# Retention in front of two feed-forward blocks: attention in native float32 by chunks of 96 tokens

## The chip, the cores and the metric

One core of a Trainium2 chip runs the whole program. The metric is the device time of one execution in microseconds (us), less is better; three runs of the kernel before have a median of 931.69 us (930.37 to 932.35).

## The reference

```python
scores = (q @ k.T) / sqrt(64)                       # 4 batches, 8 heads, 576 tokens, head size 64
gamma = 1 - 2 ** (-5 - head)
ret = scores * where(row >= col, gamma ** (row - col), 0)
x = (ret @ v)                                       # heads side by side: 2304 tokens x 512
h = max(max(x @ w1, x @ w2), x @ w3)                # 512 -> 768
x2 = h @ w_out                                      # 768 -> 512
g = x2 @ w_gate                                     # 512 -> 1536
out = (g * sigmoid(g) * (x2 @ w_val)) @ w_out2      # 1536 -> 512
```

The activations are float32 and the weights float64.

## The kernel before, in words

A product in full precision is made in one of two ways. *Native*: one matmul on float32 operands, which the profile shows as two MATMUL records (passes). *In pairs*: each operand is split into a high part that is a float32r and a float32r rest, and three matmuls (high by rest, rest by high, high by high) add up in PSUM. The feed-forward blocks work in pairs throughout.

**Conversions.** Each weight block of 128 x 512 is loaded as float64 by SP's queue (`load_w`, L86; three buffers `w64`) and turned into a float32r pair by `conv_w` (L94): two ScalarE copies (L98, L99), three VectorE steps (L100 to L102), the rounding on ScalarE (L103) and a subtraction (L104), on GpSimd for the first layer's 18 blocks and on VectorE for the others.

**Attention** works in 32 units of (batch, half of the sequence, pair of heads), halves being 256 and 320 tokens. The causal part within a half is computed over triangles of blocks (`BLK`); what the first half adds to the second goes through one 64 x 64 state per head. A unit goes through four functions:
- `a_load` (L118) loads q, k and v; from unit 12 on, q and k come in a form that VectorE can transpose.
- `a_prep` (L151) transposes q and k (TensorE L164 up to unit 11, then VectorE L168, L169), scales q by powers of the decay rate, and from unit 8 on (`NF`) splits all into float32r pairs on ScalarE, VectorE and GpSimd (L185 to L208).
- `a_score` (L211), for one head: matmuls L232, then decay and mask on VectorE (L237), then the split (L246 to L251).
- `a_value` (L254), for one head: matmuls L288, evacuation (L294 to L300, L329, L330) to the pair xh, xl, and in a first half the state (L306 to L325).

Units 0 to 7 are native. One head's matmuls use 64 of the array's 128 rows or columns; the other head's come after them.

**First layer.** `f_slice` (L357) makes a slice: 12 matmuls (L366) for one half batch, one block of 128 of h and one of the three weights, into one of three PSUM banks (`ps_mm`, L74). ScalarE copies the first of three to `hmax` (L370), VectorE takes the maximum with the other two (L372), and the result is written to DRAM (L374). There are 18 slices a half batch, 144 in all.

**Order.** The loop over the units (L405) emits preparation two units ahead, scores one ahead, values, up to three conversions for each of the first six units, and between them 4 or 5 slices a unit (`quota`, L409) from a queue that gets a half batch's 18 slices when its four units are done (L406). The last half batch's 18 slices stand behind the loop (L474 to L480), with the first conversions for the next layers. The Tile framework puts the instructions of every engine, TensorE's too, in an order by a simulated timeline, so an engine's order may leave the program's.

**Behind it**: x2 = h @ w_out by half batches, h being loaded again and split (`h_split`, L463; L498), and the second block (`gate_val` L513, `out2` L537). Both take their products from the same three `ps_mm` banks, the second block's last product from five of its own.

Of the kernel before, what the change touches and what calls it, by code (L numbers as in the profile page):

```python
# [21 lines left out]
P = 128  # L22
NP = H // 2
CH = ((0, 256), (256, 320))
C = 320
# [5 lines left out]
BLK = (((0, 128), (128, 128)), ((0, 128), (128, 128), (256, 64)))  # L31
# [3 lines left out]
O_ID, O_MK, O_SC, O_KS, O_G = 0, 128, 448, 472, 488  # L35
NCONST = O_G + NP * C


def _constants():
    """Identity, causal mask and powers of the heads' decay rates: shapes alone."""  # L40
    c = np.zeros((P, NCONST), np.float64)
    gam = 1.0 - 2.0 ** (-5.0 - np.arange(H))
    p = np.arange(P)
    m = np.arange(C)
    c[:, O_ID:O_MK] = np.eye(P)
    c[:, O_MK:O_SC] = m[None, :] >= p[:, None]
    g = np.zeros((P, NP, C))
    for pr in range(NP):
        g[:D, pr] = gam[2 * pr] ** m
        g[D:, pr] = gam[2 * pr + 1] ** m  # L50
    c[:, O_G:NCONST] = g.reshape(P, -1)
    j = 128.0 * np.arange(3)[None, :, None] + p[:, None, None]
    c[:, O_SC:O_KS] = (gam ** (-j) / np.sqrt(D)).reshape(P, -1)
    c[:, O_KS:O_G] = (gam ** (CH[0][1] - j[:, :2]) / np.sqrt(D)).reshape(P, -1)
    return c.astype(np.float32)
# [3 lines left out]
def retention_moe(ctx, tc, consts, q, k, v, w1, w2, w3, w_out, w_gate, w_val, w_out2, out):  # L59
# [14 lines left out]
    ps_mm = ctx.enter_context(tc.tile_pool(name="ps_mm", bufs=3, space=PSUM))  # L74
# [4 lines left out]
    ident = cst[:, O_ID:O_MK]  # L79
    mask = cst[:, O_MK:O_SC]  # L80
    sc_t = cst[:, O_SC:O_KS].rearrange("p (j h) -> p j h", j=3)
    ks_t = cst[:, O_KS:O_G].rearrange("p (j h) -> p j h", j=2)
    g_t = cst[:, O_G:NCONST].rearrange("p (r m) -> p r m", r=NP)

# [25 lines left out]
    NF = 8   # the first units run in native float32, the others as float32r pairs  # L110
    PT = 12  # the first units transpose on TensorE, the others on VectorE
    units = [(b, c, pr) for b in range(B) for c in range(2) for pr in range(NP)]
    NU = len(units)
    U = {}
    states = {}
    xs = {}

    def a_load(n):  # L118
        if n >= NU:
            return  # L120
        b, c, pr = units[n]
        c0, cw = CH[c]
        vn = att.tile([P, 3, 2, D], F32, name="vn", tag="vn", bufs=3)
        if n < PT:
            qk = att.tile([P, 2, 3, 2, D], F32, name="qk", tag="qk", bufs=3)
            kn = qk[:, 1, 0:2]
            nat_ld = ((qk[:, 0], q), (qk[:, 1], k), (vn, v))
        else:
            qk = att.tile([P, 2, C // 32, 32], F32, name="qk", tag="qk", bufs=3)[:, :, 0:cw // 32]
            for i, s in enumerate((k, q)):  # L130
                for e in range(2):
                    for x in range(2):
                        g = 64 * e + 32 * x
                        sp.dma_start(out=qk[g:g + 32, 1 - i],  # L134
                                     in_=s[b, 2 * pr + e, c0:c0 + cw, 32 * x:32 * x + 32].rearrange("(a p) d -> p a d", p=32))
            nat_ld = ((vn, v),)
            kn = None
            if c == 0:
                kn = att.tile([P, 2, 2, D], F32, name="kn", tag="kn", bufs=2)
                nat_ld = ((kn, k), (vn, v))  # L140
# [113 lines left out]
    def a_value(n, e):  # L254
        if n >= NU or n < 0:
            return
# [334 lines left out]
```

## Time and profile before

| | us |
|---|---|
| median of three runs | 931.69 |
| span of the profiled execution | 931.2 |
| TensorE busy (matmuls) | 898.6 |
| VectorE busy | 559.5 |
| ScalarE busy | 400.0 |
| GpSimd busy | 286.6 |

The profile gives for the profiled execution its span, from the first instruction to the last; it is the same as the runs' time within 0.5 us. Engines work beside one another, so their busy times don't add up to the span. Matmul records are pipelined and overlap: a matmul's cost is the distance from its start to the next one's start, not the length of its record. PE is TensorE's matmuls, PEld its weight loads, DVE VectorE, ACT ScalarE, POOL GpSimd, SP SyncE.

### The profile page before, as it was taken

How to read it: one execution, taken by the hardware profiler on the slowest of the kernel's cores; microseconds unless marked ns; L12 is line 12 of the kernel's file. 1: busy time of each engine (PE TensorE's matmuls, PEld its weight loads, DVE VectorE, ACT ScalarE, POOL GpSimd, SP SyncE). 2: the span in 40 equal slices, each digit the busy share in tenths (PEclk: the TensorE clock that was granted, in tenths of full speed). 3: DMA queues.
4: the chain of work that ended last, by engine and by line, in shares of the span. 5: the costliest groups of instructions: out<-in, count | busy, mean ns of one | idle time of the engine just before them, and what ended most of it. 6: DMA issues, size and time to landing. Idle time of an engine off the chain costs nothing.

```text
span 931.2 us, 14346 instructions
## 1 busy us (share of the span) xinstructions
PE 898.6 (96%) x5208; PEld 783.6 (84%) x5208; DVE 559.5 (60%) x1088; ACT 400.0 (43%) x892; POOL 286.6 (31%) x294
## 2 busy tenths in 40 slices
PE   6998988999998999999999999999999999999998
PEld 4776887989998999999988888888888888888887
DVE  3699999999999975941171154375366343333333
ACT  3666665665665755744363253143133122111111
POOL 2465435544544553144411111112111111111111
PEclk9999999999999999999999999999999999999999
DMA  7775453333232104752240021021011000000112
GB/s 174 205 209 179 86 129 67 72 70 72 62 72 61 31 25 130 236 147 83 65 130 7 1 91 45 1 91 46 1 61 53 1 1 1 1 0 1 46 68 92
DMA packets 131640, 67.79 MB, mean 73 GB/s; under 512 B 92528, under 2 KB 126960, under 8 KB 131568
## 3 DMA queue, kind: packets, MB, share of 16 engines
q1 hardware_dynamic: 131568, 66.87, 26.1%
q8 instruction: 41, 0.67, 0.3%
q14 instruction: 31, 0.25, 0.1%
HBM read 55.04 MB, written 11.80 MB: 72 GB/s over the span
## 4 chain that ended last, share of the span: by engine, by line
PE 66%; DVE 3%; DMA 2%; issue 1%; ACT 1%; SPq 0%; POOL 0%; DVEq 0%; ACTq 0%; POOLq 0%
PE ps L523 33%; PE ps L545 16%; PE ps L366 8%; PE ps L498 8%; PE o_ps L288 1%; PE s L232 1%; DMA w<-in_moe_w_val_dram 1%; DMA w<-in_moe_w_out_dram 0%; DMA qk<-in_q_dram 0%; SPq L134 0%; DVE hmax L372 0%; DVE wz L101 0%; DMA hf<-h_d 0%; DVE rq L196 0%; DVE pf L237 0%
## 5 line engine op out<-in xcount | busy, mean ns | idle before, releaser
L534 POOL TENSOR_TENSOR gl<-gf,gh 128x512 fp32r<-128x512 f32 (+1 forms) x60 | 74.7, 1245 | 385.8 <-ACT gh L533 385.8
L366 PE MATMUL ps<-xl,wh 128*128 128x256 f32 (+1 forms) x576 | 178.5, 311 | 14.7 <-DVE hmax L372 13.1
L523 PE MATMUL ps<-x2h,wrl 128*128 128x512 f32 (+1 forms) x480 | 179.1, 373 | 0.0
L523 PE MATMUL ps<-x2l,wrh 128*128 128x512 f32 (+1 forms) x480 | 179.1, 373 | 0.0
L523 PE MATMUL ps<-x2h,wrh 128*128 128x512 f32 (+1 forms) x480 | 179.1, 373 | 0.0
L366 PE MATMUL ps<-xh,wlo 128*128 128x256 f32 (+1 forms) x576 | 172.3, 299 | 0.0
L366 PE MATMUL ps<-xh,wh 128*128 128x256 f32 (+1 forms) x576 | 172.3, 299 | 0.0
L366 PEld LDWEIGHTS ps<-xl,wh 128*128 128x128 f32 x576 | 109.8, 191 | 23.2 <-DVE hmax L372 16.1
L531 DVE TENSOR_TENSOR sg<-ps,sg 128x512 f32<-128x512 f32 (+1 forms) x60 | 38.2, 637 | 125.9 <-ACT sg L530 125.7
L366 PEld LDWEIGHTS ps<-xh,wlo 128*128 128x128 f32 x576 | 110.0, 191 | 0.8 <-issue 0.8
L366 PEld LDWEIGHTS ps<-xh,wh 128*128 128x128 f32 x576 | 109.9, 191 | 0.5 <-issue 0.3
L523 PEld LDWEIGHTS ps<-x2l,wrh 128*128 128x128 f32 x480 | 90.4, 188 | 18.2
L523 PEld LDWEIGHTS ps<-x2h,wrl 128*128 128x128 f32 x480 | 90.4, 188 | 17.9
L523 PEld LDWEIGHTS ps<-x2h,wrh 128*128 128x128 f32 x480 | 90.4, 188 | 17.6
L530 ACT ACTIVATE sg<-ps 128x512 f32<-128x512 f32 (+1 forms) x60 | 33.1, 552 | 154.2 <-PE ps L523 154.1
L551 DVE TENSOR_TENSOR acc<-ps,acc 128x512 f32<-128x512 f32 x90 | 62.1, 690 | 50.7 <-PE ps L545 50.6
L247 POOL TENSOR_TENSOR pl<-pf,ph 128x384 fp32r<-128x384 f32 (+1 forms) x48 | 60.2, 1256 | 102.9 <-ACT ph L246 78.5
L533 ACT ACTIVATE gh<-gf 128x512 fp32r<-128x512 f32 (+1 forms) x60 | 35.2, 586 | 125.4 <-DVE gf L532 125.4
L545 PE MATMUL ps<-wrh,gl 128*128 128x512 f32 x216 | 85.7, 397 | 0.0
L545 PE MATMUL ps<-wrl,gh 128*128 128x512 f32 x216 | 85.5, 396 | 0.0
L545 PE MATMUL ps<-wrh,gh 128*128 128x512 f32 x216 | 85.1, 394 | 0.0
L532 DVE TENSOR_TENSOR gf<-ps,sg 128x512 f32<-128x512 f32 (+1 forms) x60 | 38.3, 638 | 65.5 <-PE ps L523 64.8
(89 smaller groups left out, 1653.7 us busy)
## 6 DMA issues: line engine op xcount, KB each, us to landing
w<-in_moe_w_dram SPq DMA_DIRECT2D x18, 512.0 KB, 4.2
w<-in_moe_w_out_dram SPq DMA_DIRECT2D x18, 512.0 KB, 4.4
w<-in_moe_w_gate_dram SPq DMA_DIRECT2D x12, 512.0 KB, 4.3
w<-in_moe_w_val_dram SPq DMA_DIRECT2D x12, 512.0 KB, 4.1
out_dram<-acc SPq DMA_DIRECT2D x18, 256.0 KB, 2.0
vn<-in_v_dram SPq DMA_DIRECT2D x64, 64.0 KB, 2.3
h_d<-hmax SPq DMA_DIRECT2D x24, 160.0 KB, 1.9
hf<-h_d SPq DMA_DIRECT2D x24, 160.0 KB, 2.5
```

Source lines behind the costliest of these rows:

```text
L232: pe.matmul(dst[i][0], lk[:, o:o + w], rq[:, o:cw], start=l == 0, stop=l == len(prods) - 1)
L247: pool.tensor_tensor(pl[:, sl], pf[:, sl], f(ph[:, sl]), ALU.subtract)
L366: pe.matmul(ps, l[:, ksl], r, start=n == 0, stop=n == 3 * KD - 1)
L498: pe.matmul(ps, l[:, es], r, start=n == 0, stop=n == 3 * F1 - 1)
L523: pe.matmul(ps[:, 0:tw], l[:, ksl], r, start=n == 0, stop=n == 3 * KD - 1)
L530: act.activation(sg[:, 0:tw], pr[0][:, 0:tw], ACTF.Sigmoid)
L531: dve.tensor_tensor(sg[:, 0:tw], pr[0][:, 0:tw], sg[:, 0:tw], ALU.mult)
L532: dve.tensor_tensor(gf[:, 0:tw], pr[1][:, 0:tw], sg[:, 0:tw], ALU.mult)
L533: act.activation(gh[:, 0:tw], gf[:, 0:tw], ACTF.Copy)
L534: pool.tensor_tensor(gl[:, 0:tw], gf[:, 0:tw], f(gh[:, 0:tw]), ALU.subtract)
L545: pe.matmul(ps, l[:, sl], r, start=n == 0, stop=n == 3 * GRP - 1)
L551: dve.tensor_tensor(a, ps, a, ALU.add)
```

## The change

- Halves are 288 and 288 tokens. Attention is native for all 32 units, now (batch, pair of heads, half), a pair's two halves one after the other. A half has three chunks of 96 tokens; scores and values are computed within a chunk, and all that came before goes through a state per chunk boundary (six states a pair, the first zero; VectorE scales the last state and adds the new product).
- Both heads' matmuls of a chunk stand one after the other in different tiles of the array: scores in the two halves of its rows, into two banks; state products and values in the two halves of its columns, into one bank. The product with the state is one matmul for both heads on a block-diagonal state.
- All transposes are on TensorE, k and q into one PSUM tile. VectorE applies decay and mask in one instruction a half and makes xl straight from PSUM.
- A pair's q, k and v (whole sequence) are loaded at once, three pairs deep. The constants come in one load.
- `ps_mm` has two banks, here and in all that follows; attention's tiles have one buffer each (six banks).
- Inside a manual schedule TensorE keeps the order in which the program emits. The slices of a batch (36, its halves alternating) join the queue when all its eight halves are done; 108 of them lie in iterations 8 to 31, the last batch's 36 behind the loop, six beside each conversion.
- `hf` has three buffers for five, `wl` two for three, `hmax` three for two, one of them held per half.

The old attention functions are left out here, as are the constants' values and comments that went.

```diff
-CH = ((0, 256), (256, 320))
-C = 320
+CK = 96
+NC = 3
+C = CK * NC
+CH = ((0, C), (C, C))
...
-O_ID, O_MK, O_SC, O_KS, O_G = 0, 128, 448, 472, 488
-NCONST = O_G + NP * C
+O_ID = 0
+O_D = O_ID + CK
+O_G = O_D + NP * 2 * CK
+O_KS = O_G + NP * CK
+O_E = O_KS + NP * 2
+NCONST = O_E + NP
...
-    ps_mm = ctx.enter_context(tc.tile_pool(name="ps_mm", bufs=3, space=PSUM))
+    ps_mm = ctx.enter_context(tc.tile_pool(name="ps_mm", bufs=2, space=PSUM))
...
-        l = stg.tile([P, 512], U32, name="wl", tag="wl")
+        l = stg.tile([P, 512], U32, name="wl", tag="wl", bufs=2)
...
+    halves = [(b, pr, h) for b in range(B) for pr in range(NP) for h in range(2)]
+    NU = len(halves)
     U = {}
     xs = {}
+    stz = [att.tile([P, 2 * NC, 2, D], F32, name=f"stz{i}", tag=f"stz{i}", bufs=1) for i in range(2)]
+    for t in stz:
+        pool.memset(t, 0.0)
+    def a_load(u):
+        if u >= B * NP:
+            return
+        b, pr = divmod(u, NP)
+        t = {}
+        for nm, s in (("k", k), ("q", q), ("v", v)):
+            t[nm] = att.tile([CK, 2 * NC, 2, D], F32, name=f"{nm}n", tag=f"{nm}n", bufs=3)
+            for e in range(2):
+                sp.dma_start(out=t[nm][:, :, e, :],
+                             in_=s[b, 2 * pr + e].rearrange("(a p) d -> p a d", p=CK))
+        U[u] = t
+    def a_prep(n):
         if n >= NU:
             return
+        b, pr, h = halves[n]
+        u = U[n // 2]
+        if h == 0:
+            ks = att.tile([CK, 2 * NC, 2, D], F32, name="ks", tag="ks")
+            sc = ks_t[:, pr].unsqueeze(1).unsqueeze(3).to_broadcast([CK, 2 * NC - 1, 2, D])
+            pool.tensor_tensor(ks[:, 0:2 * NC - 1], u["k"][:, 0:2 * NC - 1], sc, ALU.mult)
+            u["ks"] = ks
+        tp = psa.tile([P, 2, 512], F32, name="tp", tag="tp")
+        for x, nm in ((0, "k"), (1, "q")):
+            for c in range(NC):
+                pe.transpose(tp[:, x, c * CK:(c + 1) * CK],
+                             u[nm][:, h * NC + c].rearrange("p h d -> p (h d)"), ident)
+        kt = att.tile([P, C], F32, name="kt", tag="kt")
+        qg = att.tile([P, NC, CK], F32, name="qg", tag="qg", bufs=3)
+        act.activation(kt, tp[:, 0, 0:C], ACTF.Copy)
+        dve.tensor_tensor(qg, tp[:, 1, 0:C].rearrange("p (c m) -> p c m", c=NC),
+                          g_t[:, pr].unsqueeze(1).to_broadcast([P, NC, CK]), ALU.mult)
+        u[h] = {"kt": kt, "qg": qg}
+    def a_score(n):
+        if n >= NU:
+            return
+        b, pr, h = halves[n]
+        w = U[n // 2][h]
+        s = psa.tile([CK, 2, 512], F32, name="s", tag="s")
+        for c in range(NC):
+            cs = slice(c * CK, (c + 1) * CK)
             for e in range(2):
+                hd = slice(64 * e, 64 * e + 64)
+                pe.matmul(s[:, e, cs], w["kt"][hd, cs], w["qg"][hd, c], start=True, stop=True)
+        pT = att.tile([CK, 2, NC, CK], F32, name="pT", tag="pT")
+        dve.tensor_tensor(pT, s[:, :, 0:C].rearrange("p e (c m) -> p e c m", c=NC),
+                          d_t[:, pr].unsqueeze(2).to_broadcast([CK, 2, NC, CK]), ALU.mult)
+        w["pT"] = pT
+    def a_state(n):
         if n >= NU:
             return
+        b, pr, h = halves[n]
+        u = U[n // 2]
+        st = stz[(n // 2) % 2]
+        m = psa.tile([P, NC, D], F32, name="m_ps", tag="m_ps")
+        cs = [c for c in range(NC) if h * NC + c < 2 * NC - 1]
+        for c in cs:
+            g = h * NC + c
+            for e in range(2):
+                pe.matmul(m[64 * e:64 * e + 64, c], u["ks"][:, g, e], u["v"][:, g, e], start=True, stop=True)
+        for c in cs:
+            g = h * NC + c
+            for e in range(2):
+                hd = slice(64 * e, 64 * e + 64)
+                if g == 0:
+                    dve.tensor_copy(st[hd, 1, e], m[hd, c])
+                else:
+                    dve.scalar_tensor_tensor(st[hd, g + 1, e], st[hd, g, e], e_t[hd, pr:pr + 1], m[hd, c],
+                                             ALU.mult, ALU.add)
+    def a_value(n):
         if n >= NU or n < 0:
             return
+        b, pr, h = halves[n]
+        u = U[n // 2]
+        w = u[h]
+        st = stz[(n // 2) % 2]
+        o = psa.tile([P, C], F32, name="o_ps", tag="o_ps")
+        first = True
+        for c in range(NC):
+            g = h * NC + c
+            if g:
+                pe.matmul(o[:, c * CK:(c + 1) * CK], st[:, g].rearrange("p e d -> p (e d)"), w["qg"][:, c],
+                          start=first, stop=False, skip_group_check=True)
+                first = False
+        for c in range(NC):
+            g = h * NC + c
+            for e in range(2):
+                pe.matmul(o[64 * e:64 * e + 64, c * CK:(c + 1) * CK], u["v"][:, g, e], w["pT"][:, e, c],
+                          start=False, stop=True, skip_group_check=True)
+        if h == 0:
+            u["x"] = [ffn.tile([P, S], F32R, name=f"x{x}", tag=f"x{x}{pr}", bufs=2) for x in "hl"]
+        xh, xl = u["x"]
+        ts = slice(h * C, h * C + C)
+        act.activation(xh[:, ts], o, ACTF.Copy)
+        dve.tensor_tensor(xl[:, ts], o, f(xh[:, ts]), ALU.subtract)
+        xs[(2 * b + h, pr)] = (xh[:, ts], xl[:, ts])
+        if h == 1:
+            U.pop(n // 2)
...
-            mx[0] = ffn.tile([P, C], F32, name="hmax", tag="hmax", bufs=2)[:, 0:cw]
-            act.activation(mx[0], ps, ACTF.Copy)
+            mx[hb] = ffn.tile([P, C], F32, name="hmax", tag="hmax", bufs=3)[:, 0:cw]
+            act.activation(mx[hb], ps, ACTF.Copy)
         else:
-            dve.tensor_tensor(mx[0], ps, mx[0], ALU.max)
+            dve.tensor_tensor(mx[hb], ps, mx[hb], ALU.max)
         if wi == 2:
-            sp.dma_start(out=h_d[hb][fi], in_=mx[0])
+            sp.dma_start(out=h_d[hb][fi], in_=mx[hb])
...
+    sp.dma_start(out=cst, in_=consts)
     a_load(0)
+    win_load(0)
     a_load(1)
+    win_load(1)
+    wc = 0
+    pe_order = tc.manual_schedule(engines={mybir.EngineType.PE})
+    pe_order.__enter__()
+    a_prep(0)
+    win_conv(wc)
+    wc += 1
+    a_state(0)
+    a_prep(1)
     a_load(2)
+    a_score(0)
     for n in range(NU):
+        if n % 8 == 0 and n:
+            b = n // 8 - 1
+            fq += [(2 * b + h, fi, wi) for fi in range(F1) for wi in range(3) for h in range(2)]
+        if n % 2 == 0:
+            a_load(n // 2 + 3)
+        quota = (2, 1, 1, 1) if n % 2 else (1, 1, 1, 1)
+        ncv = (3 if n % 2 else 2) if n < 7 else 0
         a_prep(n + 2)
         f_some(quota[0])
+        for _ in range(ncv):
             win_conv(wc)
             wc += 1
+        a_score(n + 1)
         f_some(quota[1])
+        a_value(n)
         f_some(quota[2])
+        a_state(n + 1)
         f_some(quota[3])
+    while wc < len(win_units):
+        win_conv(wc)
+        wc += 1
+    f_some(99)
+    pe_order.__exit__(None, None, None)
...
-            hf = hw.tile([P, C], F32, name="hf", tag="hf", bufs=5)[:, 0:cw]
+            hf = hw.tile([P, C], F32, name="hf", tag="hf", bufs=3)[:, 0:cw]
...
-    hb = NHB - 1
-    fq += [(hb, fi, wi) for fi in range(F1) for wi in range(3)]
+    fq += [(2 * (B - 1) + h, fi, wi) for fi in range(F1) for wi in range(3) for h in range(2)]
     for i in range(F1):
         c2()
         h_split(0, i)
-        f_some(3)
+        f_some(6)
```

## Rows read from the trace of the kernel before

**Rows 1.** Busy time by stretch: bounds, length, then each engine (instructions), granted clock, DMA.
```profile
0.00:25.00 25.00, 17.44 (x59) 11.84 (x60) 9.73 (x29) 8.39 (x18) 6.92 (x12) 1.00 0.73 186
25.00:100.70 75.70, 72.16 (x427) 52.18 (x425) 67.66 (x115) 51.53 (x113) 42.50 (x38) 1.00 0.66 183
100.70:361.30 260.60, 244.36 (x1847) 238.33 (x1846) 233.96 (x537) 159.11 (x418) 123.02 (x135) 0.99 0.29 65
361.30:394.50 33.20, 32.22 (x218) 31.69 (x217) 28.98 (x52) 25.47 (x51) 8.60 (x10) 1.00 0.80 243
394.50:931.20 536.70, 532.42 (x2666) 449.57 (x2664) 219.21 (x359) 155.46 (x294) 105.53 (x99) 1.00 0.14 45
```

**Rows 2.** The same view of L366's matmuls alone (start and middle).
```profile
0.00:100.70 100.70, 33.52 (x216) 28.01 (x216) 1.00 0.68 184
100.70:361.30 260.60, 196.18 (x1296) 178.62 (x1297) 0.99 0.29 65
```

**Rows 3.** TensorE's longest wait from 100.7 to 361.3 us: total, times, longest.
```profile
PE ps L366 <- DVE hmax L372: 13.1, 13, 1.7
```

**Rows 4.** Timeline of TensorE, slices of 256 and 320 tokens: start, length, instruction.
```profile
53.58 0.28 PE L366 MATMUL ps<-xl,wh 128*128 128x256 f32 x1
...
54.78 0.28 PE L366 MATMUL ps<-xh,wlo 128*128 128x256 f32 x1
...
385.15 0.31 PE L366 MATMUL ps<-xh,wh 128*128 128x320 f32 x1
...
393.95 0.31 PE L366 MATMUL ps<-xh,wh 128*128 128x320 f32 x1
```

**Rows 5.** Timeline of TensorE, native groups (x4: two matmuls of two passes).
```profile
31.11 0.92 PE L232 MATMUL s<-qn,kt 64*128 64x256 f32 x4
31.96 0.64 PE L164 MATMUL tq<-cst,qk 128*128 128x128 f32 x3
...
34.72 0.63 PE L306 MATMUL m_ps<-vn,ks 128*64 128x64 f32 x8
35.27 1.13 PE L232 MATMUL s<-qn,kt 64*128 64x320 f32 x4
36.33 0.86 PE L288 MATMUL o_ps<-pf,vn 128*64 128x256 f32 x4
```

**Rows 6.** Timeline of TensorE, two native matmuls in different row tiles.
```profile
46.84 0.27 PE L232 MATMUL s<-qn,kt 64*64 64x64 f32 x1
46.85 0.27 PE L288 MATMUL o_ps<-pf,vn 64*64 64x64 f32 x1
46.95 0.22 PE L232 MATMUL s<-qn,kt 64*64 64x64 f32 x1
...
47.11 0.48 PE L288 MATMUL o_ps<-qn,st 128*64 128x320 f32 x1
```

**Rows 7.** Timeline of TensorE, one transpose, and the same with the next.
```profile
59.75 0.27 PE L164 MATMUL tq<-cst,qk 128*128 128x128 f32 x1
...
59.75 0.38 PE L164 MATMUL tq<-cst,qk 128*128 128x128 f32 x2
```

**Rows 8.** Timeline of TensorE, first transpose, and native groups before 25 us.
```profile
4.90 0.66 PE L164 MATMUL tq<-cst,qk 128*128 128x128 f32 x2 [4.90 <-DMA qk<-in_q_dram]
...
22.83 1.65 PE L232 MATMUL s<-qn,kt 64*128 64x256 f32 x4
24.41 0.69 PE L164 MATMUL tq<-cst,qk 128*128 128x128 f32 x2
```

**Rows 9.** Conversions ended (L103, ScalarE) by 41.2 us.
```profile
0.00:41.20 41.20, 2.51 (x4) 1.00 0.70 181
```

**Rows 10.** Timeline of ScalarE, the last values read of unit 3.
```profile
41.11 0.38 ACT L294 ACTIVATE xh<-o_ps 64x256 fp32r<-64x256 f32 x1 [0.36 <-PE o_ps L288]
```

**Rows 11.** VectorE's steps L101 and L102 of the first 18 conversions.
```profile
0.00:92.90 92.90, 18.21 (x18) 1.00 0.70 192
...
0.00:92.90 92.90, 16.68 (x18) 1.00 0.70 192
```

More of the change, by code (lines that the diff above doesn't have):

```diff
@@ L107, in cols @@
         return w[:, c0:c0 + P].rearrange("(a p) n -> p a n", p=P)
[L110 to L113, printed above, removed]
+    halves = [(b, pr, h) for b in range(B) for pr in range(NP) for h in range(2)]
+    NU = len(halves)
     U = {}
-    states = {}
     xs = {}
-    def a_load(n):
-        if n >= NU:
-            return
[L121 to L140, printed above, removed]
-        for t, s in nat_ld:
-            for e in range(2):
-                sp.dma_start(out=t[:, 0:2, e, :],
-                             in_=s[b, 2 * pr + e, c0:c0 + 256, :].rearrange("(a p) d -> p a d", p=P))
-            if cw > 256 and t is not kn:
-                for x in range(2 if t is vn and n >= NF else 1):
-                    sp.dma_start(out=t[64 * x:64 * x + 64, 2, :, :],
-                                 in_=s[b, 2 * pr:2 * pr + 2, c0 + 256:c0 + cw, :].rearrange("h p d -> p h d"))
-        U[n] = {"qk": qk, "kn": kn, "vn": vn}
@@ L194, in a_prep @@
-        for e, (a, o) in enumerate(((lo, up), (up, lo))):
-            act.activation(rq[e][a], qs[a], ACTF.Copy)
-            dve.tensor_tensor(rq[e][o], qs[a], f(rq[e][a]), ALU.subtract)
-        vv = att.tile([P, 3, 2, 2, D], F32R, name="vv", tag="vv", bufs=3)
-        bb = slice(0, 2 + c)
-        act.activation(vv[:, bb, :, 0, :], vn[:, bb], ACTF.Copy)
-        pool.tensor_tensor(vv[:, bb, :, 1, :], vn[:, bb], f(vv[:, bb, :, 0, :]), ALU.subtract)
-        u.update(rq=rq, lk=lk, vv=vv, p=[None, None])
@@ new lines, in a_state @@
+    def a_state(n):
+        if n >= NU:
+            return
[17 more added lines that the diff above has]
+                                             ALU.mult, ALU.add)
@@ L212, in a_score @@
+    def a_value(n):
         if n >= NU or n < 0:
             return
-        b, c, pr = units[n]
-        u = U[n]
-        if n < NF:
-            hd = slice(64 * e, 64 * e + 64)
-            prods = [(u["lk"][hd], u["rq"][hd])]
-        else:
-            prods = [(u["lk"][e][:, l], u["rq"][e]) for l in range(2)]
-        cw = CH[c][1]
-        s = psa.tile([P, 512], F32, name="s", tag="s", bufs=3)
-        dst, off = [], 0
-        for i, (o, w) in enumerate(BLK[c]):
-            n_ = cw - o
-            if off + n_ > 512:
-                s2 = psa.tile([64, 64], F32, name="s2", tag="tp", bufs=2)
-                dst.append((s2, off, n_))
-            else:
-                dst.append((s[0:w, off:off + n_], off, n_))
-            for l, (lk, rq) in enumerate(prods):
-                pe.matmul(dst[i][0], lk[:, o:o + w], rq[:, o:cw], start=l == 0, stop=l == len(prods) - 1)
-            off += n_
@@ new lines, in a_value @@
+        b, pr, h = halves[n]
[12 more added lines that the diff above has]
+            g = h * NC + c
+            for e in range(2):
+                pe.matmul(o[64 * e:64 * e + 64, c * CK:(c + 1) * CK], u["v"][:, g, e], w["pT"][:, e, c],
+                          start=False, stop=True, skip_group_check=True)
@@ L472, in h_split @@
             hsp[(i, fi)] = (hh, hl)
-    hb = NHB - 1
-    fq += [(hb, fi, wi) for fi in range(F1) for wi in range(3)]
+    fq += [(2 * (B - 1) + h, fi, wi) for fi in range(F1) for wi in range(3) for h in range(2)]
     for i in range(F1):
```

211 lines of the change are left out of this document (14 added, 197 removed).

## The prediction

> **What bounds the kernel now.** I cut the span where the first layer's work changes pace and read each stretch by itself [rows 1]. To 100.7 us (the start) no engine is full from the first instruction on: TensorE is busy 17.4 of the first 25 us, and VectorE fills up only after 25 us. From 100.7 to 361.3 us (the middle) TensorE is busy 244.4 of 260.6 us and VectorE 234.0: both are nearly full. From 361.3 to 394.5 us (the tail) and in all that follows TensorE is busy almost without a gap, so a microsecond saved or lost ahead of 394.5 us moves the end by a microsecond, and the 536.7 us behind it stay as they are unless the banks (below) touch them.
>
> The second view counts the first layer's matmuls in the same stretches [rows 2]: 216 in the start and 1296 in the middle, which is 18 and 108 slices of 12, and by the program's count 18 of the 144 are left for the tail. So in the start eight units of attention and one half batch of slices are done, in the middle 24 units and six half batches. In the middle TensorE's longest wait in sum is for VectorE's maximum, 13.1 us [rows 3].
>
> A slice is priced by its pace, not by the duration of a record. At 256 tokens ten matmuls start in 1.20 us, 0.120 us each; at 320 sixty start in 8.80 us, 0.147 us each [rows 4]. The 108 slices of the middle, half of either kind, take 54 x 12 x (0.120 + 0.147) = 172.8 us, and the other 87.8 us are 24 units: **3.66 us for a unit**, with TensorE's idle 16.2 us (0.68 us a unit) in it.
>
> **The change part by part.** After it the same three stretches can be told apart, and the middle is the same sum: iterations 8 to 31 carry 24 half pairs and 108 slices. A slice of 288 tokens lies halfway, 12 x 0.133 = 1.60 us, so the slices of the middle take 172.8 us again.
>
> *A half pair in native float32.* Each native matmul is two records (passes). Four score passes over 768 columns take 0.85 us from their start to the next group's, four over 1024 take 1.06 us [rows 5]; the difference gives 0.82 ns a column, and what is left, 0.22 us, is paid once at the entry to a group of another tile shape. Eight state passes of 64 columns take 0.55 us, of which by the same pace 0.42 is columns and 0.13 entry. So a pass of 96 columns is 0.08 us and one of 64 is 0.055 to 0.06.
> Two heads in two array tiles have one example: a score and a value matmul of 64x64 start 0.01 us apart, and the group behind them starts 0.27 us after the first [rows 6]. One after the other, four passes of 64 and the entry would be 0.35 to 0.46 us. Two row tiles thus overlap fully. Two column tiles occur nowhere in the trace: between full overlap and none I take full, because those row tiles are the nearest row.
> - Transposes: the second starts 0.11 us after the first (0.38 less 0.27) [rows 7]. Six: 0.66 us.
> - Scores: 12 passes of 0.08, in pairs: 0.48 us (0.96 without overlap).
> - State products: on average 5 matmuls, 10 passes of 0.06, in pairs: 0.30 us (0.60).
> - Values from the state: 2.5 matmuls on 128 weight columns, 5 passes at the 0.11 of the transposes, which also load 128 columns: 0.55 us.
> - Values within a chunk: 12 passes, in pairs: 0.48 us (0.96).
> - Six changes of tile shape in an iteration (slice to score and back, state values to chunk values, back to a slice, slice to state and back), each 0.13 to 0.22 us, so 0.18: 1.08 us.
> Sum 3.55 us against 3.66: 24 x 0.11 = **-2.6 us**. That has no idle time; I add 0.1 us a half, **+2.4 us**. VectorE can't be the cover that goes: an iteration issues 8 of its instructions for attention and 3 maxima instead of 537 / 24 = 22, at the middle's mean of 0.44 us [rows 1] 4.8 us of 10.7.
>
> *The start.* Slices now wait for the whole of batch 0, eight halves, so TensorE does attention alone. In the old start its attention ran at half pace: four score passes over 768 columns took 1.58 us [rows 8] against 0.85 later, 1.86 times as long, although natives followed one another closely; the column of the granted clock doesn't show it. I take this lower level (1.2 GHz) for the whole start. A half without the two entries to slices is 3.55 - 0.36 = 3.19 us, times 1.86 is 5.9; eight are 47.5 us, and two more halves' transposes with one more score and state step, done ahead, are 2.1 x 1.86 = 3.9. The old start packed TensorE to 17.4 of the 20 us behind its first transpose at 4.9 us [rows 1, 8]: 51.4 / 0.87 + 5 = 64 us. **64 - 100.7 = -36.7 us.** The weights' 18 conversions need not be over by then: in the old start 4 were done by 41.2 us [rows 9], when the last values of unit 3 were read [rows 10], though 12 stand ahead of them in program order. The ends: 50 us if the clock rises early, and 90 us if all 18 conversions go first. Two of the three VectorE steps of one cost 1.01 and 0.93 us [rows 11], 35 us for 18; the third and 28 us for eight halves (8 x 8 x 0.44) are nearly the 77.4 us VectorE was busy in the old start [rows 1].
> The larger constants load (one transfer ahead of the first transpose) lies within the 5 us, give or take 1; SP's waiting loads of the fourth and later pairs hold up nothing that is due within 20 us.
> [...]
>
> *The tail.* 36 slices of 1.60 are 57.6 us in place of 33.2: **+24.4 us**. The conversions of the next weights, loads of h and their splits have 24 us more to hide in.
>
> *Two banks in place of three* for every product behind the slices, to the end of the kernel. The only price in the trace is the 13.1 us that TensorE waits for the maximum with three banks and a VectorE 90% busy [rows 1, 3]; with VectorE half empty I take **+3 us**, ends 0 and 13.
>
> The other edits (order of slices by two halves, fewer buffers for the split h and the conversion, zeroed state tiles) lie beside TensorE's work: nothing.
>
> Sum: -36.7 + 2.0 - 2.6 + 2.4 + 24.4 + 3.0 = -7.5 us. The profiled span is 931.2 us, the median of the runs 931.7; I set the sum against the latter: **924 us**.
>
> **The rivals.**
> 1. *Column tiles don't overlap* (the change doesn't do what it says for values and states). A half costs 0.78 us more, 24 x 0.78 = 18.7 us in the middle and up to 0.78 x 1.86 x 8 / 0.87 = 13 us in the start, as far as conversions don't hide it: 943 to 956, about 950. It decides from a quarter of the overlap lost (0.3 us a half eats the 7.5). For it: no row with two column tiles. Against it: the row tiles.
> 2. *All conversions first*: VectorE runs them ahead of the attention and the start lasts 90 us: +26, 950. Against it: the old start's order [rows 9, 10].
> 3. *A short start*, about 52 us, by a clock that rises early or closer packing: 912.
> 4. *Passes start strictly in program order.* Then the first pass of the second head can't start before the second pass of the first, and every paired group has one pass more: 0.08 + 0.06 + 0.08 = 0.22 us a half, 5.3 us in the middle and 3 in the start: 932. Rows 6 speak against it: the value matmul's first pass starts at 46.85, the score's second at 46.95. The Trainium skill (TensorE: Matmul & The Clock Gate, Part 3: Packing small matmuls) states that rule, matmuls being in program order at start and end with no reordering; by it the time would be the 932 of this rival.
>
> **How the numbers follow.** Chances: the forecast 0.45 (its own range 914 to 934), rival 1 0.20, rival 2 0.15, rival 3 0.15, rival 4 0.05. Below 907 and above 950 lies what the range leaves out: the far half of rivals 1 and 2 and the best of rival 3. A measurement tells 0.2% (1.9 us) from no change. Faster: 0.35 of the forecast's 0.45 and rival 3, 0.50. Same: 0.06 of the forecast's and half of rival 4, 0.09. Slower: rivals 1 and 2 and what is left, 0.41.
>
> **What would show it.** In the new profile: the first slice at about 64 us and 18 conversions not yet over; scores of two heads starting within 0.02 us of one another, and so for states and values (if these start 0.08 us or more apart throughout, rival 1); 24 iterations of 10.8 us; VectorE under half busy in the middle; 36 slices back to back of 1.6 us; behind them the same 537 us. Wrong it would be by a first slice beyond 75 us, by TensorE waiting on a maximum or an evacuation for more than 0.3 us a slice, or by a half above 4 us.

## The result, and the profile after

The changed kernel takes 936.91 us (936.13 to 937.73, five runs) beside 931.69 (928.36 to 932.35) for the one before: a ratio of 1.0074 [1.0054, 1.0093]. It is **slower by 0.7%** where 924 us and faster had been forecast; the time lies inside the range. The profiled execution spans 935.1 us, 3.9 more than before.

Busy time of the changed kernel by stretch, columns as in [rows 1]: until about the first slice (two rows), the first 12 slices, the other 96 of the middle, the tail, all behind it.

```profile
0.00:25.00 25.00, 15.42 (x120) 12.86 (x122) 11.56 (x24) 6.95 (x13) 7.87 (x11) 1.00 1.16 228
25.00:71.70 46.70, 36.31 (x289) 29.84 (x285) 44.31 (x83) 25.63 (x48) 19.39 (x14) 1.00 0.82 205
71.70:111.10 39.40, 31.70 (x272) 29.21 (x270) 31.28 (x58) 15.15 (x30) 9.44 (x7) 0.91 0.53 143
111.10:333.10 222.00, 222.00 (x2069) 207.77 (x2066) 91.31 (x231) 32.19 (x78) 12.44 (x11) 1.00 0.20 53
333.10:395.40 62.30, 60.01 (x434) 57.60 (x433) 40.40 (x75) 28.06 (x54) 8.57 (x8) 1.00 0.50 160
395.40:935.10 539.70, 533.50 (x2666) 449.11 (x2664) 212.78 (x349) 154.94 (x291) 106.02 (x99) 1.00 0.14 43
```

Against the terms of the forecast:

| stretch | before | forecast | after | after less forecast |
|---|---|---|---|---|
| start, to the first slice (before: with 18 slices in it) | 100.7 | 64.0 | 71.7 | +7.7 |
| middle, 108 slices, the sum's 2.0 us for the clock in it | 260.6 | 262.4 | 261.4 | -1.0 |
| tail, 36 slices | 33.2 | 57.6 | 62.3 | +4.7 |
| behind it | 536.7 | 536.7 | 539.7 | +3.0 |
| two banks, place not named | | 3.0 | (in the two rows above) | -3.0 |
| span | 931.2 | 923.7 | 935.1 | +11.4 |

The middle is right only in sum. Two stretches of eight iterations, 36 slices each, that overlap by a third take 84.5 us apiece (the next view; one iteration is 10.56 us where 10.8 were forecast); 24 iterations at that pace would be 253.5. But the first 12 slices took 39.4 us and not the 28.2 of that pace, 11.2 more, and the other 96 took 222.0 and not 225.3, since the last iterations have no next halves to prepare.

```profile
111.10:195.60 84.50, 84.50 (x796) 78.93 (x792) 34.77 (x89) 11.50 (x28) 5.00 (x4) 1.00 0.25 64
167.10:251.60 84.50, 84.50 (x796) 78.91 (x793) 34.77 (x89) 11.50 (x28) 5.00 (x4) 1.00 0.25 64
```

**The start and the first slices.** TensorE's waits up to 112 us (total, times, longest), the changed kernel:

```profile
PE ps L258 <- DVE hmax L264: 5.8, 1, 5.8
PE o_ps L208 <- DVE xl L221: 5.6, 3, 3.5
PE o_ps L208 <- DVE stz L193: 4.6, 7, 1.1
PE tp L149 <- DVE qg L154: 2.3, 1, 2.3
```

All of these, 18.3 us, wait for VectorE, which is busy 44.31 of 46.70 us from 25 us to the first slice. Its costliest groups from 0 to 90 us (count, busy, mean ns, idle before) are the three steps of the conversions, 18 of the first layer and the first step of a nineteenth:

```profile
L105 DVE SCALAR_TENSOR_TENSOR wz<-w,wz 128x512 uint32<-128x512 uint32 x18 | 18.9, 1049 | 0.4
L104 DVE TENSOR_SCALAR wz<-wz 128x512 uint32<-128x512 uint32 x19 | 15.5, 815 | 0.7 <-ACT wz L102 0.5
L106 DVE CUSTOM_DVE_ANT_0 wl<-wz,wl 128x1024 uint16<-128x1024 uint16 x18 | 14.4, 799 | 0.7
```

48.8 us of 90. The same forms in the same execution from 540 to 900 us, where GpSimd has little to do, are shorter:

```profile
L106 DVE CUSTOM_DVE_ANT_0 wl<-wz,wl 128x1024 uint16<-128x1024 uint16 x21 | 15.2, 730 | 1.9 <-ACT wl L103 1.8
L105 DVE SCALAR_TENSOR_TENSOR wz<-w,wz 128x512 uint32<-128x512 uint32 x19 | 13.4, 705 | 0.2
L104 DVE TENSOR_SCALAR wz<-wz 128x512 uint32<-128x512 uint32 x19 | 8.0, 419 | 0.8 <-ACT wz L102 0.5
```

The long ones lie beside GpSimd's instructions. Timeline of VectorE, then of GpSimd (start, length), at the worst place:

```profile
80.63 0.42 DVE L104 TENSOR_SCALAR wz<-wz 128x512 uint32<-128x512 uint32 x1
...
81.76 1.70 DVE L105 SCALAR_TENSOR_TENSOR wz<-w,wz 128x512 uint32<-128x512 uint32 x1
83.59 0.69 DVE L106 CUSTOM_DVE_ANT_0 wl<-wz,wl 128x1024 uint16<-128x1024 uint16 x1
84.20 0.42 DVE L104 TENSOR_SCALAR wz<-wz 128x512 uint32<-128x512 uint32 x1
84.66 0.69 DVE L105 SCALAR_TENSOR_TENSOR wz<-w,wz 128x512 uint32<-128x512 uint32 x1
85.49 1.53 DVE L106 CUSTOM_DVE_ANT_0 wl<-wz,wl 128x1024 uint16<-128x1024 uint16 x1
86.94 2.70 DVE L104 TENSOR_SCALAR wz<-wz 128x512 uint32<-128x512 uint32 x1
89.93 0.44 DVE L264 TENSOR_TENSOR hmax<-ps,hmax 128x288 f32<-128x288 f32 x1
```

```profile
85.03 1.45 POOL L108 TENSOR_TENSOR wlo<-wl,wh 128x512 fp32r<-128x512 f32 x1 [2.12 <-ACT wh L107]
86.44 1.70 POOL L144 TENSOR_TENSOR ks<-kn,cst 96x640 f32<-96x640 f32 x1
88.10 1.26 POOL L108 TENSOR_TENSOR wlo<-wl,wh 128x512 fp32r<-128x512 f32 x1
```

Step L104, 0.42 us by itself, lasts from 86.94 to 89.64, until the last GpSimd instruction ends at 89.36. The maximum for which TensorE waits 5.8 us (L264, at 89.93) stands behind it. Its slice's last record had ended at 80.42, so it stood 9.5 us, 8.2 of them behind the seven conversion steps from 80.63 on. At their lengths without GpSimd (0.42 for L104, 0.68 for the others) the seven would take 4.0 us, so of the 9.5 about 4 go with the order and about 4 with the longer steps (an estimate). The step at 86.94 isn't even the first layer's: all 18 of that kind had run by 84.62, and it is the first of the next layers' weights, put here by the planner.

The Trainium skill (SBUF — State Buffer, "SBUF: two separate sides") says that VectorE and GpSimd share a pair of ports that one instruction holds to its end while the other is blocked, for VectorE's operations with two SBUF inputs or in a two-port mode. The trace agrees: over the whole execution L104 takes 0.96 us in the mean where its record overlaps a GpSimd instruction's (17) and 0.42 where it doesn't (43), L105 1.14 (18) and 0.68 (42), L106 0.89 (24) and 0.68 (36); the maximum, one of whose inputs is in PSUM, takes 0.45 (5) and 0.46 (91). Which of the two cases L104 with its one input is, no run shows.

While TensorE waits, its granted clock falls. Windows of 10 us, same columns as the first view: TensorE is busy 3.15 of the 10 us from 80 us, and the mean granted clock is 0.87 and 0.79, one stretch at the lower level (1.2 GHz) from 87.4 to 94.2 us. The column has a limit: the clock records in the trace begin at 73.8 us only, 2.1 behind the start of the first slice, and a stretch without a record counts as 1.00 (in the kernel before they begin at 29.3 us [rows 1]).

```profile
70.00:80.00 10.00, 9.57 (x84) 8.82 (x82) 9.59 (x19) 6.38 (x12) 3.96 (x3) 1.00 0.77 202
80.00:90.00 10.00, 3.15 (x30) 2.67 (x28) 9.64 (x11) 6.29 (x12) 5.78 (x4) 0.87 0.53 157
90.00:100.00 10.00, 9.57 (x71) 9.10 (x72) 8.61 (x21) 2.26 (x5) 0.00 (x0) 0.79 0.80 193
```

**Two heads side by side.** Timeline of TensorE in the middle, the groups of one half and the slice behind (the score group starts 0.68 us ahead of what follows, the transposes 0.44):

```profile
155.09 0.41 PE L149 MATMUL tp<-cst,kn 96*128 96x96 f32 x3
155.34 0.41 PE L149 MATMUL tp<-cst,qn 96*128 96x96 f32 x3
155.53 0.38 PE L258 MATMUL ps<-xl,wh 128*128 128x288 f32 x1
...
158.89 0.75 PE L168 MATMUL s<-qg,kt 64*96 64x96 f32 x12
159.57 0.40 PE L258 MATMUL ps<-xl,wh 128*128 128x288 f32 x1
```

The starts of the score records, taken one by one from the trace: they come in pairs 0.007 us apart, the second pair 0.160 us behind the first and the others every 0.085 us. A record doesn't name its head; that the two of a pair are the two heads is read from the spacing, as the passes of one head emitted alone (run 4) start 0.160 and then 0.085 us apart. Below are the scores (row tiles), then the first pairs of values and of state products (column tiles), which start the same way.

```
158.887  158.894 | 159.047  159.054 | 159.132  159.139 | 159.217  159.224 | 159.302  159.309 | 159.387  159.394
161.999  162.006 | 162.133  162.139 | 162.215  162.222
164.427  164.434 | 164.534  164.540 | 164.592  164.599
```

**The tail.** TensorE shows little idle time ahead of the slices there (records overlap, so a late start hides in part), but its pace is 62.3 / 36 = 1.73 us a slice, not 1.60, and the wait is for the evacuation by VectorE and ScalarE. A maximum starts 0.70 us in the mean (1.76 at most) behind the last record of its slice, where in the 96 slices before it is 0.06:

```profile
L258 PE MATMUL ps<-xl,wh 128*128 128x288 f32 x144 | 43.6, 303 | 2.3 <-DVE hmax L264 1.4 <-ACT hmax L262 0.7
```

### The profile page after: what moved, and what is told of

The parts are those of the page before. It is cut to its first block, busy times and chain, and to the rows that moved or that the text cites. A ratio compares the mean times of both kernels' runs of the same rounds, so it can differ in the third digit from the quotient of the medians.

```text
span 935.1 us, 14209 instructions
## 1 busy us (share of the span) xinstructions
PE 898.9 (96%) x5832; PEld 786.4 (84%) x5832; DVE 431.6 (46%) x816; ACT 262.9 (28%) x512; POOL 163.7 (18%) x148
## 4 chain that ended last, share of the span: by engine, by line
PE 84%; DVE 7%; DMA 3%; issue 2%; ACT 2%; POOL 1%; SPq 0%; POOLq 0%; DVEq 0%; ACTq 0%
PE ps L406 31%; PE ps L258 22%; PE ps L428 15%; PE ps L381 7%; DVE wz L105 2%; PE o_ps L214 2%; PE s L168 2%; PE o_ps L208 2%; PE tp L149 1%; DVE wz L104 1%; DVE wl L106 1%; PE m_ps L185 1%; DMA h_d<-hmax 1%; DMA w<-in_moe_w_gate_dram 1%; DVE stz L193 1%
## 5 line engine op out<-in xcount | busy, mean ns | idle before, releaser
L258 PE MATMUL ps<-xl,wh 128*128 128x288 f32 x576 | 181.4, 315 | 9.6 <-DVE hmax L264 7.2
L258 PE MATMUL ps<-xh,wlo 128*128 128x288 f32 x576 | 170.8, 297 | 0.0
L258 PE MATMUL ps<-xh,wh 128*128 128x288 f32 x576 | 170.5, 296 | 0.0
L413 ACT ACTIVATE sg<-ps 128x512 f32<-128x512 f32 (+1 forms) x60 | 33.2, 554 | 166.6 <-PE ps L406 166.6
L264 DVE TENSOR_TENSOR hmax<-ps,hmax 128x288 f32<-128x288 f32 x96 | 43.8, 456 | 76.4 <-PE ps L258 71.9
L355 POOL TENSOR_TENSOR hl<-hf,hh 128x288 fp32r<-128x288 f32 x48 | 40.4, 860 | 143.3 <-ACT hh L354 142.3
```

What stands on the lines that cost most here:

```text
L258: pe.matmul(ps, l[:, ksl], r, start=n == 0, stop=n == 3 * KD - 1)
L264: dve.tensor_tensor(mx[hb], ps, mx[hb], ALU.max)
L355: pool.tensor_tensor(hl, hf, f(hh), ALU.subtract)
L413: act.activation(sg[:, 0:tw], pr[0][:, 0:tw], ACTF.Sigmoid)
```

## The experiments

The theory after the comparison: the start and the first slices are set by VectorE's conversions (cost about 13 us), and two banks cost the tail and what follows about 6; the heads' overlap works. Rivals: TensorE's low clock or the weights' transfers set the start whatever VectorE does; the banks cost nothing; the overlap isn't needed. The expectations name each theory by a letter of its own. Runs 1, 4, 6 and 7 are single executions. The runs were made on several chips, on which the kernel before took 929.1 to 931.7 us (medians), so differences of about 2 us between runs are not told apart.

**1. VectorE's load taken away.** Two of its three steps left out in the first layer's 18 conversions.

```diff
-        dve.tensor_scalar(z, z, 3, None, ALU.logical_shift_left)
-        dve.scalar_tensor_tensor(z, u[:, :, 1], 0x80000000, z, ALU.bitwise_and, ALU.bitwise_or)
+        if not light:                        # light for the first layer's blocks
+            dve.tensor_scalar(z, z, 3, None, ALU.logical_shift_left)
+            dve.scalar_tensor_tensor(z, u[:, :, 1], 0x80000000, z, ALU.bitwise_and, ALU.bitwise_or)
```

> The changed kernel, but two of the three VectorE steps of each of the first layer's 18 conversions are left out (the shift and the sign, 35 us of VectorE up to 90 us; the weights are then not the right ones); loads, ScalarE and GpSimd steps stay. Theory V (VectorE's conversions fill the start, attention and slices wait in its queue): the first slice comes at 52 to 58 us instead of 71.7, TensorE has no gap between 72 and 96 us, the time is 909 to 917 us. Rival C (TensorE at its lower clock sets the start): first slice at 62 to 66 us, 929 to 935 us. Rival D (the weights' transfers set it): the eighteenth conversion still ends at 85 to 90 us, 927 to 935 us.

Measured: 923.48 us; first slice at 63.3 us in place of 71.7, the first 12 slices in 34.1 us, no stretch at the lower clock from 65.0 us on, where its clock records begin. That is 13.4 us less than the changed kernel, so VectorE is what set the end there. The 18th conversion is rounded at 71.9 us in place of 87.1, so the weights' transfers aren't the bound (rival D). The time lies between the ranges of theory V and of rival C, and the first slice is in rival C's, no earlier than the forecast's 64: another bound stands right behind VectorE.

**2. Conversions later in the program.**

```diff
-        ncv = (3 if n % 2 else 2) if n < 7 else 0
+        ncv = 1 if n < 7 else 2 if n < 12 else 0
```

> The changed kernel with the same work, but the first layer's conversions are emitted later: one in each of iterations 0 to 6 and two in each of 7 to 11, instead of two or three in each of 0 to 6. Theory V: attention of batch 0 is through VectorE's queue sooner, the first slice comes at 55 to 60 us, the remaining conversions lie beside slices, 919 to 927 us. Rival C (TensorE's lower clock): first slice at 64 us or later, 931 to 936 us. Rival D (transfers): no change, 935 to 938 us.

Measured: 935.04 us (933.62 to 936.78, ten runs), ratio to before 1.0061 [1.0041, 1.0082]. The first slice comes at 69.1 us, and the 18th conversion is rounded at 86.4 where it was at 87.1. The 1.9 us are not clear of the spread, and theory V's 919 to 927 is missed. Moving the emission alone hardly moved VectorE's work: its order is the planner's, not the program's (run 8 fixes it).

**3. Three banks again behind attention.**

```diff
     psa_cm.__exit__(None, None, None)
     att_cm.__exit__(None, None, None)
+    psm_cm.__exit__(None, None, None)
+    ps_mm = ctx.enter_context(tc.tile_pool(name="ps_mm3", bufs=3, space=PSUM))
```

> The changed kernel with three PSUM banks again for everything behind the attention (last 36 slices, x2, second block); two within the attention. Theory B (the two banks leave too little time for an evacuation behind a conversion): the last 36 slices take 58 us instead of 62.5, what follows 537 instead of 539.5, 930 to 932 us. Rival H (the three buffers for h and their writes to DRAM, held up by weight loads, set the gaps): the last 36 slices take 61 us or more, 935 to 938 us.

Measured: 930.63 us (929.90 to 931.61, ten runs), ratio 1.0017 [0.9998, 1.0036]: 6.3 us less (5.3 by the two ratios), about what the change had lost. Tail and what follows in this run:

```profile
335.30:393.20 57.90, 57.51 (x432) 57.27 (x433) 38.98 (x72) 26.96 (x53) 7.07 (x7) 1.00 0.54 166
393.20:928.60 535.40, 531.76 (x2666) 449.12 (x2664) 213.90 (x349) 155.70 (x291) 105.17 (x99) 1.00 0.14 44
```

4.4 us come from the tail, which is now the 57.6 forecast, and 4.3 from behind it; 2.2 are lost ahead of the tail, where the banks change hands (at the 109th slice). What two banks cost among the first slices, where TensorE waited 5.8 us for one, no run measured.

**4. Head by head.** The loops over chunks and heads exchanged in scores, states and values, so one head's matmuls come first.

```diff
-        for c in range(NC):
-            cs = slice(c * CK, (c + 1) * CK)
-            for e in range(2):
+        for e in range(2):
+            for c in range(NC):
+                cs = slice(c * CK, (c + 1) * CK)
```

> The changed kernel with the matmuls of scores, states and values emitted head by head (three chunks of one head, then three of the other) instead of chunk by chunk with the two heads side by side. If heads overlap only when their matmuls stand next to one another: most of the overlap is lost, a half costs 0.5 to 0.8 us more, the middle stretch 12 to 19 us, 950 to 960 us. If TensorE reaches past six matmuls for another tile: 935 to 939 us.

Measured: 950.37 us, 13.5 more. The same group of 12 score passes lasts 1.00 us to the end of its records where it lasted 0.75:

```profile
163.03 1.00 PE L168 MATMUL s<-qg,kt 64*96 64x96 f32 x12
```

From start to the next start it is 0.93 us and was 0.68; a half's values take 0.86 (0.65), its states 0.53 in the mean (0.44). The overlap is real, for column tiles too, and most of it needs the heads' matmuls next to each other.

**5. The conversions' subtraction on VectorE instead of GpSimd** (with three banks).

```diff
-        conv_w(win_ld.pop(i), hi, lo, pool)
+        conv_w(win_ld.pop(i), hi, lo)
```

> Three banks behind attention as in the run with three banks (930.6 us), and the last step of each first-layer conversion on VectorE instead of GpSimd. Theory P (VectorE's conversion steps last 0.82, 1.03 and 0.80 us up to 87 us because GpSimd works beside them; the same forms are shorter later, where no GpSimd subtraction of this size runs): VectorE's work falls although it gets 18 more steps, the first slice comes at 64 to 68 us and the time is 924 to 928. Theory W (the steps' lengths have nothing to do with GpSimd): 18 steps of some 0.7 us more on the engine that sets the start, the first slice at 76 to 82 us where it now stands at 71.7, and 936 to 943 us.

Measured: 919.57 us (919.42 to 920.34, four runs), ratio 0.9883 [0.9861, 0.9905]. VectorE's conversion steps from 0 to 90 us, now four:

```profile
L106 DVE SCALAR_TENSOR_TENSOR wz<-w,wz 128x512 uint32<-128x512 uint32 x19 | 14.4, 760 | 0.1
L107 DVE CUSTOM_DVE_ANT_0 wl<-wz,wl 128x1024 uint16<-128x1024 uint16 x19 | 14.0, 739 | 0.2
L109 DVE TENSOR_TENSOR wlo<-wl,wh 128x512 fp32r<-128x512 f32 x18 | 12.3, 685 | 0.3
...
L105 DVE TENSOR_SCALAR wz<-wz 128x512 uint32<-128x512 uint32 x20 | 9.4, 471 | 0.2
```

The three old steps fell from 2.66 to 1.97 us together (0.815 + 1.049 + 0.799 against 0.471 + 0.760 + 0.739), which pays for the fourth of 0.685. The time is below theory P's range and the first slice later than its 68 us. The gain lies where the long step was: the maximum for which TensorE had waited 5.7 us is waited for 1.7 us in all, the clock is at 2.4 GHz from 71.3 us on, and the first slice (69.0 us) begins 12 slices that take 31.8 us in place of 39.8 (run 3). The planner's order changed with the edit too, so the run doesn't part the shorter steps from it.

**6. TensorE asked for slice-like work early**, on top of run 1.

```diff
+    def warm(k):
+        ps = ps_mm.tile([P, C], F32, name="ps", tag="mm")
+        for i in range(k):
+            pe.matmul(ps, wu[:, 0:P], wu, start=i == 0, stop=i == k - 1)
...
         f_some(quota[0])
+        if n < 8:
+            warm(8)                          # and again behind the values
```

> Leaves out two of VectorE's three steps in the first-layer conversions, as the run without them (923.5 us, first slice 63.3), and adds 128 matmuls of 288 columns of the sliced type with an unread result among the passes of the first eight halves, so that TensorE is asked for such work before the first slice. Theory C (what stands behind VectorE is TensorE at its 1.2 GHz level): the granted clock is 1.0 well before 63 us, native passes at half their length from there on, the first slice at 52 to 60 us although up to 15 to 30 us of matmuls were added. Theory D (transfers or the chain of passes stand behind it): the clock rises early too, but the first slice comes at 63 us or later by what was added, up to 75 us.

Measured: 922.05 us, first slice 65.6. Native groups of the start: the changed kernel's scores, then this run's.

```profile
63.38 1.28 PE L168 MATMUL s<-qg,kt 64*96 64x96 f32 x12
```

```profile
50.25 0.75 PE L169 MATMUL s<-qg,kt 64*96 64x96 f32 x12
```

The same 12 passes last 1.28 us without and 0.75 with slice-like work around them. The clock records of this run begin at 19.5 us, those of the changed kernel behind its first slice, and run 11 has 1.28 us for this group in a stretch granted 0.50. So TensorE did run at the pace of its lower level in front of the first slice. 128 x 0.133 = 17 us of matmuls were added, and the first slice comes 2.3 us later than in run 1, with TensorE's waits 1.6 us shorter: most of what was added, the higher clock paid for. That is theory D's case; nothing is left of the gain at the first slice.

**7. TensorE's order left to the planner** (the manual schedule removed, otherwise the changed kernel).

> The changed kernel without TensorE's order written by hand. Theory O (the order as written is what keeps the two heads' passes side by side and fills the slices between): the middle's 216 slices take longer than the 261.4 us they take now, by 5 us or more, and the time is 942 to 960. Theory N (the planner would find as good an order): 934 to 940.

Measured: 941.55 us. (The 261.4 us of the expectation are those of 108 slices, not 216.) The time falls just short of theory O's range. The first slices now stand between the groups of batch 0 (first at 27.3 us), the 12th is done at 102.5 in place of 111.1; but 36 slices of the middle take 89.8 us where they took 84.5, and 96 take 235.4 in place of 222.0. The order by hand is worth some 5 us in sum, in the middle.

**8. VectorE's order fixed too, conversions later** (runs 2 and 3 with VectorE in the manual schedule).

```diff
-    pe_order = tc.manual_schedule(engines={mybir.EngineType.PE})
+    pe_order = tc.manual_schedule(engines={mybir.EngineType.PE, mybir.EngineType.DVE})
```

> Three banks behind attention (930.6 us), the first-layer conversions emitted one per half up to the seventh and two per half up to the twelfth, and VectorE's order kept as written too, not TensorE's alone. Theory E (the start is long because VectorE takes conversions ahead of the steps that attention's next passes wait for): the first slice comes at 50 to 62 us, later conversions ride in the middle, where VectorE is busy 41% of the time, and the total is 915 to 926. Theory F (a VectorE bound to one order waits at its head for other engines, and the slices then wait on it): the first slice is no earlier than 66 us or the middle grows by 5 us or more, 930 to 950.

Measured: **917.89 us** (917.28 to 919.32, four runs), ratio 0.9864 [0.9836, 0.9892], the fastest of all. First slice 64.3 us, the next 12 in 33.4, the 18th conversion at 108.5. The time is in theory E's range, the first slice 2 us behind it. TensorE's waits for VectorE up to the first slice; of those for xl and stz only 0.2 us are left:

```profile
PE tp L150 <- DVE qg L155: 4.1, 1, 4.1
PE s L169 <- DVE pT L171: 2.3, 3, 2.0
```

With run 2 this shows the order at work: the same later emission changes the time by 1.9 us where VectorE's order is the planner's, and it gains 12.7 beside run 3 where it is the program's. The program's order with the old emission was not run.

**9. Runs 5 and 8 together.**

> Both at once: three banks, first-layer conversions later with VectorE's order as written (917.9 us), and their last step on VectorE instead of GpSimd (919.6 us with three banks alone). If the two gains have separate causes (order, and steps lengthened beside GpSimd), the first slice comes at 59 to 62 us and the time is 911 to 915 us; if both remove the same wait, VectorE's load in front of the first slices, it is 916 to 921 us: the steps put off no longer lie ahead of the first slice, and the 18 more steps of VectorE stand in its written order ahead of slices' evacuations.

Measured: 931.80 us (930.89 to 934.0, ten runs), ratio 1.0029 [1.0012, 1.0045]; worse than either and outside both theories. VectorE's waits up to 125 us:

```profile
DVE wlo L109 <- ACT wh L108: 13.3, 17, 1.7
DVE qg L155 <- ACT kt L154: 13.2, 3, 9.6
```

17 times it stands at the subtraction's head until ScalarE has rounded, with attention's steps behind it in the written order; TensorE waits 6.8 us for pT and 9.0 for the maximum.

**10. As 9, the subtraction half an attention step later.** It is put in a list and emitted behind the next half's preparation.

> As the run with both at once (931.8 us), but the last step of a first-layer conversion stands one half of attention later in VectorE's written order. Theory Q (what spoiled the run with both was that VectorE, bound to its order, stood 13.3 us at this step's head waiting for ScalarE's rounded weights, with the steps of attention behind it): that wait falls below 3 us, the first slice comes at 59 to 65 us and the time is 910 to 917 us, at or below the 917.9 us of the run with the order alone. Theory R (VectorE's 18 more steps themselves are too much for the stretch): 923 to 932 us, the first slice at 67 us or later.

Measured: 921.88 us (920.17 to 924.31, eight runs), ratio 0.9932 [0.9910, 0.9953]. The wait is gone from VectorE's list, and 9.9 us with it, so that wait spoiled run 9. But it isn't the 917 expected: the first slice is at 69.4 us, as theory R had it, TensorE still waits 6.7 us for pT, and the time lies between the two ranges. Each theory has half: the order's wait counts, and what is left against run 8 (4.0 us) goes with the 18 more steps.

**11. Slice-like work early, with VectorE off the path** (run 8, and 64 matmuls as in run 6).

> The run with VectorE's order as written and three banks (917.9 us, first slice 64.3), with 64 matmuls of 288 columns of the sliced type (an unread result) among the first eight halves. They add 64 x 0.133 = 8.5 us of TensorE's time. Theory C again, now with VectorE off the path: what is left in front of the first slice is TensorE at its 1.2 GHz level, natives fall to half their length once such matmuls run (a group of 12 score passes from 1.28 to 0.75 us), the first slice comes at 50 to 60 us and the total at 905 to 914 us. Theory G: another engine stands right behind, the first slice is at 62 us or later and the total 916 to 926 us.

Measured: 918.13 us (917.33 to 922.54, four runs), ratio 0.9896 [0.9861, 0.9932], first slice 66.3: no gain, theory G's case. The mean granted clock of 30 to 60 us, and the score groups there:

```profile
30.00:60.00 30.00, 26.85 (x249) 22.28 (x247) 21.34 (x54) 12.20 (x25) 8.78 (x7) 0.77 0.72 163
```

```profile
36.07 0.75 PE L169 MATMUL s<-qg,kt 64*96 64x96 f32 x12 [0.88 <-DVE pT L171]
38.89 0.96 PE L209 MATMUL o_ps<-qg,stz 128*128 128x96 f32 x4 [2.07 <-DVE xl L222]
...
46.11 1.28 PE L169 MATMUL s<-qg,kt 64*96 64x96 f32 x12
...
53.57 0.75 PE L169 MATMUL s<-qg,kt 64*96 64x96 f32 x12
```

The passes fall to 0.75 us. From 34 to 40 us TensorE is busy 2.86 of 6 us, with waits for VectorE of 0.88 and 2.07; then come 13.7 us at the lower level (from 39.8 us), and they are 1.28 again until 53.5. What was gained early is lost there. Whether the start could go below 60 us with a clock that stays up was not tried further.

## Why the prediction was wrong

**The start: the step that failed** is VectorE's conversions, which the sum puts at nothing there. "The old start packed TensorE to 17.4 of the 20 us behind its first transpose" was carried over to eight halves, and VectorE's sum ("35 us for 18; the third and 28 us for eight halves ... are nearly the 77.4 us") was set beside 64 us and passed by, since conversions "need not be over by then". TensorE's share was right: with VectorE lightened or ordered the first slice comes at 63.3 and 64.3 us (runs 1 and 8). But VectorE takes conversions ahead of what attention waits for, as rival 2 had it, in part: 13 of 18 are rounded before the first slice, and it came at 71.7, not 90.

**The clock and the first slices.** The sum has 2.0 us for the clock at the first slices; no run shows that term as it stands. The trace shows a clock record from 2.1 us behind the first slice's start on, and a first slice of 2.78 us to the end of its last record where the second has 1.86, about 1 us (an estimate from these two). But the first 12 slices cost 11.2 us more than their pace, and most of that is waiting, which was put at nothing: VectorE still had the first layer's conversions until 87 us and then one of the next layers', some of them lengthened beside GpSimd; TensorE waited 5.8 us behind them for a maximum and 1.5 for ScalarE, and in that long wait the clock fell. With the start's 7.7, and less the 2.0 in the sum, that makes 16.9 us; runs 1, 5 and 8 took back 11 to 13 of them.

**Two banks** were priced at 3 us, ends 0 and 13; run 3 measured 6.3, in the tail and behind it: right in kind, half the size. The rows of the wait for the maximum [rows 3] were the right place for the bound; the reason for the low choice, a VectorE half empty, doesn't hold in the tail, where VectorE is busy 40.4 of 62.3 us with conversions too, and a maximum starts 0.70 us behind its slice and not 0.06.

**A half** came out cheaper: with 4.5 slices of 1.60 us, 7.20, an iteration of 10.56 leaves 3.36 us in place of 3.65 with the idle time; the six transposes alone took 0.44 and not 0.66. That gave 24 x 0.29 = 7 us, and the missing preparation at the end, not in the sum, 3.3. These hid most of the 11.2 us above: that the middle came out within 1.0 us is luck.

**Right**: heads side by side (rivals 1 and 4 fall by the starts 0.007 us apart, in row and in column tiles, and by run 4); VectorE at 91.3 of 222.0 us in the middle; the slice of 1.6 us; the tail at 57.9 us with three banks. The rule that rival 4 takes pass by pass from the Trainium skill (TensorE: Matmul & The Clock Gate, Part 3: Packing small matmuls), matmuls in program order at start and end, is not what the trace shows of passes: by the spacing, the second head's first pass starts ahead of the first head's second. Rival 3's short start didn't come: the clock rose early only with slice-like work added (runs 6 and 11), and the first slice was no earlier for it. Of the marks set for a wrong forecast, a first slice beyond 75 us didn't come; a wait of more than 0.3 us a slice for a maximum or an evacuation did, at the first 12 slices (5.8 and 1.5 us).

## What to carry to other kernels

When a change takes one engine's work out of a stretch, add up the others' work in the shortened stretch, by the durations they have with their neighbours running, and look in which order a planner will put it: work that isn't due can stand ahead of work that is. Fixing a second engine's order can be worth more than the change (here 12.7 us together with later conversions, where the change lost 5.2), but an instruction that waits for a third engine must then stand where its input is ready. Price the loss of a PSUM bank by the stretch where the evacuating engine has other work, not by the mean.

## What the runs showed of the hardware that was not expected

VectorE's conversion steps, which read SBUF, were 0.21 to 0.54 us longer in the mean where they overlapped a GpSimd instruction, and one of 0.42 us lasted 2.70; a maximum, which reads PSUM and SBUF, was not longer (0.45 and 0.46). Native float32 passes ran at half pace (12 scores in 1.28 us, not 0.75) for some 70 us of the changed kernel, ahead of the first clock record, until slices or matmuls of that type stood among them; the granted clock of 1.00 shown for that time is no record. In the changed kernel the clock fell 2.8 us into a wait of 5.8 us and stayed at 1.2 GHz for 6.8; in run 11, after 6 us with TensorE busy 2.86 of them, for 13.7. And passes of two array tiles overlap in part even head by head: in the middle of run 4's score group pairs of records start 0.004 to 0.006 us apart (163.275 and 163.281, 163.441 and 163.445).
